# Pinned instruction order, constant matmuls at the start and moved bound work in a fused attention and FFN kernel

## Chip, core, metric

One core of one Trainium2 chip. The metric is the device time of one execution in microseconds (us). A profile gives the span from the first to the last instruction, some 1.8 us below the time (1.7 to 2.4 us).

Engines are named as in the profile: PE is TensorE, DVE is VectorE, ACT is ScalarE, SP is SyncE, which issues nearly all transfers, and POOL is GpSimd.

## The reference

```python
def _A_ref(x, k_cache, v_cache, wq, wo):       # 32 query heads, 4 kv heads, last W = 512 keys
    q = (x @ wq).reshape(B, Sq, 32, 128)...    # x is 2048 x 1024
    scores = einsum('bhqd,bhkd->bhqk', q, k) * Dh ** (-0.5)
    p = _softmax(scores, axis=-1)
    return (p @ v).reshape(B, Sq, 4096) @ wo
def _B_ref(x, w_gate, w_up, w_down):           # 1024 -> 3584 -> 1024
    return silu(x @ w_gate) * (x @ w_up) @ w_down

mod = (_silu(c) @ w_mod).reshape(...)          # sa, ca, ga, sb, cb, gb
h = _layernorm(x) * (1 + ca) + sa
x = x + ga * _A_ref(h, ...)
h = _layernorm(x) * (1 + cb) + sb
x = x + gb * _B_ref(h, ...)
```

All inputs are bf16.

## The kernel before

The 2048 rows are worked in four chunks of 512. The attention part is one loop of 128 steps, one head of one chunk each. In a step TensorE computes the scores of head `k`, the Q projection of head `k + 3`, the output of head `k - 1`, and one piece of the output projection of finished heads. Everything else hangs on a table of tasks by step: `at(k, f, ...)`. After the loop comes the FFN, chunk by chunk.

```python
def put_q(g, q_ps):                            # VectorE empties PSUM; the scores of head g need it
    t = wk.tile([P, TCW], BF16, name="qT", tag="row", bufs=5)
    nc.vector.tensor_copy(out=t, in_=q_ps)
    qT[g] = t
...
def load_rb(g):                                # 1/rowsum, written to DRAM by ScalarE's queue (r_d), read back
    for i in range(2):                         # broadcast to all partitions
        rb = wk.tile([P, 2, TCW], FP32, name="rb", tag="rb", bufs=2)
        nc.sync.dma_start(out=rb, in_=d[2 * i:2 * i + 2, :].partition_broadcast(P))
def emit_norm(g):
    for i, rb in enumerate(rinv.pop(g // 4)):
        nc.vector.tensor_tensor(out=oo, in0=oo, in1=rb, op=ALU.mult)   # oT <- oT, rb
...
def plan_ln(k, key, sc, sh):                   # layernorm of one chunk, spread over steps
    for t in range(QT):
        tt = key[1] * QT + t
        at(k + 2 * t, ln_stats, tt)            # VectorE statistics, ScalarE Ln and Exp
        at(k + 2 * t + 1, ln_rows, tt)         # VectorE: xn
        at(k + 2 * t + 2, ln_xpose, key, tt)   # transposing transfer hT <- xn on the SP queue
    for dt in range(DT):
        at(k + 11 + dt, ln_mod, key, dt, sc, sh)   # VectorE: hT <- hT * scale + shift
...
for hg in range(H // 4):                       # bound work: sums of squares of wq and k, for a check
    for i in range(2):                         # that the scores can't overflow without a row maximum
        for j in range(2):
            at(max(0, 4 * hg - 3 + 2 * i + j), bound_wq, hg, i, j)
at(6, load_k)
at(10, bound_k)                                # 16 products, one after the other
...
for k in range(NU + 1):                        # NU = 128
    if k % 4 == 2 and k + 6 < NU:
        load_wq((k + 6) // H, ((k + 6) % H) // 4)
    if k < NU: emit_s(k)
    if k + LEAD < NU: emit_q(k + LEAD)
    ...
    run_tasks(k)
    if k >= 1:
        if k % 4 == 0: emit_l(k - 1)
        emit_o(k - 1)
```

Between this source and the chip stands a scheduler. It reorders the instructions of each engine, and the transfers of the SP queue, by its own estimate of when their inputs will be ready. Each engine then works through the resulting list.

## Time and profile before

| | before |
|---|---|
| median time at first (3 runs) | 1295.99 us (1292.82 to 1296.79) |
| profiled span | 1293.1 us |
| first Q matmul / first scores matmul | 15.44 / 28.15 us |
| from first scores to the end | 1264.95 us |
| PE idle in windows of 5 us: 70-80 us / 175-185 us | 1.42 / 1.23 us |

The page says at once what the bound is. First the busy time of TensorE and its share of the span, then the shares of the chain that ended last:

```profile
PE 1274.6 (99%) x6169; PEld 575.1 (44%) x6169; DVE 653.4 (51%) x1144; ACT 454.0 (35%) x646; POOL 0.7 (0%) x6
...
PE 93%; DVE 4%; DMA 1%; issue 1%; ACT 0%; SPq 0%; DVEq 0%
```

TensorE is the bound, and in steady state a 128x512 matmul starts every 0.2158 us. This is the chain of waits, start, duration and what ran: 448 matmuls in 96.69 us.

```profile
852.56 96.69 PE gu_ps L1099 x448
```

So a change can win only the start and the few stretches in which TensorE idles. The busy time by stretches shows those (stretch, its length, then for each engine the busy us with the number of instructions in brackets, then the granted clock, DMA share and GB/s):

```profile
70.00:75.00 5.00, 4.22 (x22) 1.67 (x20) 5.00 (x39) 2.43 (x3) 0.00 (x0) 1.00 1.08 275
75.00:80.00 5.00, 4.36 (x19) 1.60 (x19) 5.00 (x9) 3.75 (x5) 0.00 (x0) 1.00 1.23 354
175.00:180.00 5.00, 3.90 (x19) 1.66 (x17) 3.65 (x8) 2.43 (x3) 0.00 (x0) 1.00 0.99 311
```

At 70-80 us VectorE is full; at 175-180 us it is not. The start, in the timeline (start us, duration us, engine, line, operation, output and inputs, forms, and the idle time before it with what ended it):

```profile
15.44 2.72 PE L878 MATMUL q_ps<-hT,wq 128*128 128x512 bf16 x6 [0.44 <-ACT hT L826]
...
18.07 2.28 PE L878 MATMUL q_ps<-hT,wq 128*128 128x512 bf16 x6
...
21.31 0.94 PE L728 MATMUL mod_ps<-siluc,wm_1_119 128*128 128x1 bf16 x32 [0.25 <-DVE modT L730]
...
23.53 4.27 PE L878 MATMUL q_ps<-hT,wq 128*128 128x512 bf16 x12
...
28.15 1.02 PE L966 MATMUL s_ps<-qT,kT 128*128 128x512 bf16 x4
```

Twelve Q matmuls run from 15.44 us, then two groups of w_mod columns, then twelve more Q matmuls, then the first scores. Six in 2.72 us with pipelined ends is 0.43 us apart, twice the steady 0.216. The Trainium skill, "TensorE: Matmul & The Clock Gate", Part 1, describes this: the array starts at half clock and gets the full one after about 3.4 us of sustained work. The granted clock that the profile prints for 10-20 us here is 1.00 all the same: no clock event was on record yet, so near the start the spacing of matmuls is the better witness. The trace also keeps the times at which the granted clock changed (views of narrow windows show them). The first such record here is a step to full clock at 19.77 us, 4.33 us after the first Q matmul. The second is a fall back to half from 23.18 to 26.60 us, and that is why the second twelve Q matmuls take 4.27 us (clock 0.82, third from the end):

```profile
20.00:25.00 5.00, 4.50 (x71) 2.74 (x70) 1.84 (x8) 1.55 (x2) 0.00 (x0) 0.82 1.03 188
```

Last, what VectorE waited for between 28 and 690 us that was a transfer (total us, times, longest us):

```profile
DVE oT L1004 <- DMA rb<-r_d: 18.8, 16, 1.7
DVE hT L829 <- DMA hT<-xn: 12.1, 5, 5.9
...
DVE xn L809 <- DMA hT<-xn: 2.1, 1, 2.1
```

With one wait of 1.3 us more these make 34 us.

### The profile page before, as it was taken

What the parts mean: (1) busy time and instruction counts of PE and PEld (TensorE: products, weight loads), DVE (VectorE), ACT (ScalarE), POOL (GpSimd) and SP (SyncE); (2) the same over time, 40 slices, a digit from 0 to 9 for tenths busy, and PEclk for the clock granted to TensorE, in tenths of its full rate; (3) what the DMA queues carried; (4) which work ended last, traced back from release to release, by engine and by line L of the source; (5) the groups of instructions that cost most, each with busy time, mean ns of one, the idle gap of its engine ahead of it and who ended that gap; (6) DMA issues with size and microseconds to landing.
All of it is one profiled execution on the core that took longest, in us unless ns stands there. A gap on an engine that the chain in (4) does not pass through costs nothing.

```text
span 1293.1 us, 15465 instructions
## 1 busy us (share of the span) xinstructions
PE 1274.6 (99%) x6169; PEld 575.1 (44%) x6169; DVE 653.4 (51%) x1144; ACT 454.0 (35%) x646; POOL 0.7 (0%) x6
## 2 busy tenths in 40 slices
PE   6999999999999999999999999999999999999998
PEld 3444444444444444444444444444444444444444
DVE  5999768975569655597654641221222211222122
ACT  3755545655455555555453441001100111011100
POOL 0000000000000000000000000000000000000000
PEclk9999999999999999999999999999999999999999
DMA  9897584665354645355447475453536445454402
GB/s 303 273 320 215 206 203 144 187 172 177 122 184 137 180 139 172 130 156 171 163 137 232 161 224 180 145 191 131 165 105 215 167 144 180 137 191 131 147 18 83
DMA packets 219939, 221.08 MB, mean 171 GB/s; under 512 B 45385, under 2 KB 205129, under 8 KB 219858
## 3 DMA queue, kind: packets, MB, share of 16 engines
q1 hardware_dynamic: 214690, 215.54, 52.6%
q10 hardware_dynamic: 5168, 4.46, 1.0%
q8 instruction: 50, 0.82, 0.2%
q14 instruction: 31, 0.25, 0.1%
HBM read 207.63 MB, written 4.47 MB: 164 GB/s over the span
## 4 chain that ended last, share of the span: by engine, by line
PE 93%; DVE 4%; DMA 1%; issue 1%; ACT 0%; SPq 0%; DVEq 0%
PE gu_ps L1099 30%; PE a_ps L1031 17%; PE d_ps L1119 15%; PE q_ps L953 15%; PE o_ps L1014 8%; PE s_ps L966 7%; DVE junk L893 1%; PE l_ps L983 1%; PE q_ps L878 1%; DVE psA L973 1%; DVE qT L855 1%; DMA rb<-r_d 1%; DVE st L793 0%; DMA hT<-xn 0%; DVE psB L975 0%
## 5 line engine op out<-in xcount | busy, mean ns | idle before, releaser
L968 ACT ACTIVATE pT<-s_ps 128x1024 bf16<-128x1024 f32 x256 | 249.0, 1028 | 8.7 <-PE s_ps L966 5.3
L1031 PE MATMUL a_ps<-wo,oT 128*128 128x512 bf16 x1024 | 242.3, 379 | 1.7 <-DVE qT L855 1.2
L953 PE MATMUL q_ps<-hT,wq 128*128 128x512 bf16 x1000 | 237.1, 380 | 0.3 <-DVE modT L730 0.3
L1104 ACT ACTIVATE sg<-gu_ps 128x512 bf16<-128x512 f32 x112 | 66.9, 597 | 460.4 <-PE gu_ps L1099 306.6
L1105 DVE TENSOR_TENSOR guT<-gu_ps,sg 128x512 bf16<-128x512 f32 x112 | 77.5, 692 | 280.8 <-ACT sg L1104 280.8
L1099 PE MATMUL gu_ps<-hT,wu 128*128 128x512 bf16 x896 | 211.8, 379 | 0.0
L1099 PE MATMUL gu_ps<-hT,wg 128*128 128x512 bf16 x896 | 211.7, 379 | 0.0
L1119 PE MATMUL d_ps<-wd,guT 128*128 128x512 bf16 (+2 forms) x952 | 194.2, 367 | 0.0
L1031 PEld LDWEIGHTS <-oT 128*128 128x128 bf16 x1024 | 99.6, 98 | 123.8 <-issue 2.8
L1016 ACT CAST oT<-o_ps 128x512 bf16<-128x512 f32 x128 | 74.3, 580 | 226.3 <-PE o_ps L1014 226.3
L953 PEld LDWEIGHTS <-wq 128*128 128x128 bf16 x1000 | 97.6, 98 | 118.3 <-issue 0.3
L1119 PEld LDWEIGHTS <-guT 128*128 128x128 bf16 x952 | 90.7, 98 | 103.1
L1099 PEld LDWEIGHTS <-wg 128*128 128x128 bf16 x896 | 87.5, 98 | 105.8
L1099 PEld LDWEIGHTS <-wu 128*128 128x128 bf16 x896 | 87.4, 98 | 106.0 <-DMA wu<-in_B_w_up_dram 0.4
L966 PE MATMUL s_ps<-qT,kT 128*128 128x512 bf16 x512 | 131.8, 379 | 0.6 <-ACT pT L968 0.6
L1014 PE MATMUL o_ps<-pT,v_sb 128*128 128x512 bf16 x512 | 131.8, 380 | 0.0
L973 DVE TENSOR_TENSOR psA<-pT 128x1024 bf16<-128x1024 bf16 x128 | 88.2, 689 | 72.5 <-ACT pT L968 72.3
L855 DVE CAST qT<-q_ps 128x512 bf16<-128x512 f32 x128 | 87.8, 688 | 52.9 <-PE q_ps L953 50.7
L1004 DVE TENSOR_TENSOR oT<-oT,rb 128x1024 bf16<-128x1024 bf16 x64 | 78.0, 1223 | 20.6 <-DMA rb<-r_d 20.5
L966 PEld LDWEIGHTS <-kT 128*128 128x128 bf16 x512 | 50.0, 98 | 61.5 <-issue 1.3
L1014 PEld LDWEIGHTS <-v_sb 128*128 128x128 bf16 x512 | 47.3, 98 | 61.7 <-issue 9.0
L975 DVE TENSOR_TENSOR psB<-psA 128x512 bf16<-128x512 bf16 x128 | 53.8, 421 | 0.6
(267 smaller groups left out, 454.2 us busy)
## 6 DMA issues: line engine op xcount, KB each, us to landing
wq<-in_A_wq_dram SPq DMA_DIRECT2D x64, 512.0 KB
rb<-r_d SPq DMA_DIRECT2D x64, 512.0 KB
wo<-in_A_wo_dram SPq DMA_DIRECT2D x64, 512.0 KB
wg<-in_B_w_gate_dram SPq DMA_DIRECT2D x56, 512.0 KB
wu<-in_B_w_up_dram SPq DMA_DIRECT2D x56, 512.0 KB
wd<-in_B_w_down_dram SPq DMA_DIRECT2D x56, 512.0 KB
wmr<-in_w_mod_dram SPq DMA_DIRECT2D x8, 1024.0 KB
out_dram<-o_sb ACTq DMA_DIRECT2D x31, 128.0 KB
```

Of the source, the lines that this page charges most:

```text
L855: nc.vector.tensor_copy(out=t, in_=q_ps)
L953: nc.tensor.matmul(q_ps, lhsT=wq_tiles[(cc, h // 4, dt // 4)][:, dt % 4, (h % 4) * P:(h % 4 + 1) * P], rhs=hT[("h1", cc)][:, dt, :], start ...
L966: nc.tensor.matmul(s_ps[:, i, :], lhsT=kT[:, kv, j * P:(j + 1) * P], rhs=qT[g], start=True, stop=True)
L968: nc.scalar.activation(out=p[:, 2 * jj:2 * jj + 2, :], in_=s_ps, func=ACT.Exp, scale=scale)
L973: nc.vector.tensor_tensor(out=a, in0=p[:, 0:2, :], in1=p[:, 2:4, :], op=ALU.add)
L1004: nc.vector.tensor_tensor(out=oo, in0=oo, in1=rb, op=ALU.mult)
L1014: nc.tensor.matmul(o_ps, lhsT=v_sb[:, kv, j, :], rhs=pT[g][:, j, :], start=(j == 0), stop=(j == WT - 1))
L1016: nc.scalar.copy(out=oT[(cc, hg)][:, hi, :], in_=o_ps)
L1031: nc.tensor.matmul(a_ps, lhsT=oT[(cc, 2 * q + i)][:, hh % 4, t * P:(t + 1) * P], rhs=wo_tiles[(cc, q, dh, i)][:, hh % 4, :], start=(hh == ...
L1099: nc.tensor.matmul(ps[:, n, :], lhsT=gu_w[(cc, fg, nm, dt // 4)][:, dt % 4, fi * P:(fi + 1) * P], rhs=hT[("h2", cc)][:, dt, :], start=(dt ...
L1105: nc.vector.tensor_tensor(out=guT[(cc, fg)][:, fi, :], in0=ps[:, 1, :], in1=g, op=ALU.mult)
L1119: nc.tensor.matmul(d_ps, lhsT=guT[(cc, f // 4)][:, f % 4, t * P:(t + 1) * P], rhs=wd_tiles[(cc, dh, f // 4)][:, f % 4, c0:c0 + w], start=( ...
```

## The change

Its intent: hold the clock of TensorE up while the first loads land; take the bound work out of chunk 0, where VectorE is full; and stop the scheduler from putting transfers, and VectorE work that waits for transfers, earlier than they can run. `keep_in_program_order` adds an order edge from an instruction to the one traced just before it on its engine. It sets the order of issue only and is no wait.

```diff
+    stage = {"dma": True, "steps": False}
+    def pin(ins, what="steps"):
+        return tc.keep_in_program_order(ins) if stage[what] else ins
+    def fetch(out, in_):                       # every load of the attention part goes through this
+        pin(nc.sync.dma_start(out=out, in_=in_), "dma")
...
+    def warm(n):                               # constants
+        for _ in range(n):
+            tc.keep_in_program_order(
+                nc.tensor.matmul(warm_ps, lhsT=ones_bf, rhs=warm_w, start=True, stop=True))
+    warm(16)
...                                             # in the first layernorm, after each transpose group:
+        warm(2)
...                                             # pinned VectorE work: bn_stats, xn, hT modulation,
-            nc.vector.tensor_tensor(out=oo, in0=oo, in1=rb, op=ALU.mult)     # bound products, norm
+            pin(nc.vector.tensor_tensor(out=oo, in0=oo, in1=rb, op=ALU.mult))
...
-                at(max(0, 4 * hg - 3 + 2 * i + j), bound_wq, hg, i, j)
-    at(6, load_k)
-    at(10, bound_k)
+                at((1 + hg % (NTC - 1)) * H + max(0, 4 * hg - 3 + 2 * i + j), bound_wq, hg, i, j)
+    at(NU - H + 2, load_k)
+    for kv in range(Hkv):
+        at(NU - H + 20 + 2 * kv, bound_k, kv)
...
+    def plan_late_ln(k, key, sc, sh):          # only for the last chunk's second layernorm
+        for t in range(QT):
+            tt = key[1] * QT + t
+            at(k + 2 * t, late_stats, tt)
+            at(k + 10 + 2 * t, ln_rows, tt)
+            at(k + 11 + 2 * t, ln_xpose, key, tt)
+        at(k + 8, late_rstd)                   # one 1/sqrt for all four row tiles, on VectorE
...
+    stage["steps"] = True
     for k in range(NU + 1):
...                                             # wq, wo and w_mod loads are also split over two steps;
...                                             # output projection and 2nd layernorm come one step later
+    stage.update(dma=False, steps=False)       # before the FFN
```

More of the change, by code (lines that the diff above doesn't have):

```diff
@@ L653, in big, with load @@
         return psp.tile(list(shape), dt, name=name, tag="s", bufs=2)
-    def load(out, in_, eng=None):
+    stage = {"dma": True, "steps": False}
[3 more added lines that the diff above has]
+        pin(nc.sync.dma_start(out=out, in_=in_), "dma")
+    def load(out, in_):
         with nc.allow_non_contiguous_dma(reason="weight slice"):
-            (eng or nc.sync).dma_start(out=out, in_=in_)
+            fetch(out=out, in_=in_)
     nc.scalar.preload_act_table_set("natural_log_exp_and_others")
@@ L666, in load_x @@
     def load_x(tt):
-        nc.sync.dma_start(out=xt[tt], in_=x2d[tt * P:(tt + 1) * P, :])
+        fetch(out=xt[tt], in_=x2d[tt * P:(tt + 1) * P, :])
     wm_tiles = {}
@@ L691, in fast_path @@
     for kv in range(Hkv):
-        nc.sync.dma_start_transpose(out=kT[:, kv, :], in_=A_k_cache[0, kv, k0:k0 + W, :])
+        pin(nc.sync.dma_start_transpose(
+            out=kT[:, kv, :], in_=A_k_cache[0, kv, k0:k0 + W, :]), "dma")
     v_sb = blkB("v_sb", [P, Hkv, WT, Dh])
@@ L704, in fast_path @@
     nc.vector.memset(eps_t, eps)
+    warm_w = const.tile([P, 512], BF16, name="warm_w")
+    nc.gpsimd.memset(warm_w, 0.5)
+    warm_ps = mm("warm_ps")
+    def warm(n):
[3 more added lines that the diff above has]
+    warm(16)
     modT = const.tile([P, 4, DT], FP32, name="modT")
@@ L742, in fast_path, with load_rows @@
     row_d = {}
-    def load_rows(vecs, part):
-        wm_rows.append([])
-        for vec in vecs:
-            t = hpool.tile([P, 4, D], BF16, name="wmr", tag="hT")
-            load(t, wm_v[:, 4 * part:4 * part + 4, vec * D:(vec + 1) * D])
-            wm_rows[-1].append(t)
+    def load_rows(vec, part):
+        t = hpool.tile([P, 4, D], BF16, name="wmr", tag="hT")
+        load(t, wm_v[:, 4 * part:4 * part + 4, vec * D:(vec + 1) * D])
+        wm_rows.append(t)
     def mod_rows(n, part):
         ps = mm("row_ps")
-        tiles = wm_rows.pop()
+        tiles = [wm_rows.pop(0) for _ in range(2)]
         for k in range(4):
@@ L766, in mod_rows @@
             d = dp.tile([4, TCW], FP32, name="row_d", tag="row_d", bufs=2)
-            nc.sync.dma_start(out=d, in_=r[0:P:32, :])
+            fetch(out=d, in_=r[0:P:32, :])
             row_d[n] = d
     def load_gate(n, k, dst):
-        nc.sync.dma_start(out=dst.rearrange("p (a b) -> p a b", a=2),
+        fetch(out=dst.rearrange("p (a b) -> p a b", a=2),
                           in_=row_d[n][k:k + 2, :].partition_broadcast(P))
@@ L776, in load_cols @@
         with nc.allow_non_contiguous_dma(reason="1024 values to columns"):
-            nc.sync.dma_start(out=dst, in_=src)
+            fetch(out=dst, in_=src)
         if add_one:
@@ L788, in fast_path, with ln_stats @@
     ln = {}
-    def ln_stats(tt):
+    def ln_stats(tt, late=None):
         st = sm.tile([P, DH, nc.vector.BN_STATS_DIM], FP32, name="st", tag="st")
         for i in range(DH):
-            nc.vector.bn_stats(out=st[:, i, :], in_=xt[tt][:, i * 512:(i + 1) * 512])
+            pin(nc.vector.bn_stats(out=st[:, i, :], in_=xt[tt][:, i * 512:(i + 1) * 512]))
+        if late is not None:
+            nc.vector.bn_aggr(out=late[:, 0:2], in_=st)
+            return
         mv = sm.tile([P, 4], FP32, name="mv", tag="mv", bufs=4)
@@ L808, in ln_norm @@
         else:
-            nc.vector.tensor_scalar(out=n, in0=xt[tt], scalar1=mv[:, 0:1], scalar2=mv[:, 2:3],
-                                    op0=ALU.subtract, op1=ALU.mult)
+            pin(nc.vector.tensor_scalar(out=n, in0=xt[tt], scalar1=mv[:, 0:1],
+                                        scalar2=mv[:, 2:3], op0=ALU.subtract, op1=ALU.mult))
         return n
@@ L821, in ln_xpose @@
             new_hT(key)
-        nc.sync.dma_start_transpose(out=hT[key][:, :, t * P:(t + 1) * P], in_=xn.pop(tt))
+        pin(nc.sync.dma_start_transpose(
+            out=hT[key][:, :, t * P:(t + 1) * P], in_=xn.pop(tt)), "dma")
     def ln_affine(key, dt, ps, sc, sh, on_act):
@@ L828, in ln_affine @@
         else:
-            nc.vector.tensor_scalar(out=hT[key][:, dt, :], in0=ps, scalar1=sc[:, dt:dt + 1],
-                                    scalar2=sh[:, dt:dt + 1], op0=ALU.mult, op1=ALU.add)
+            pin(nc.vector.tensor_scalar(out=hT[key][:, dt, :], in0=ps, scalar1=sc[:, dt:dt + 1],
+                                        scalar2=sh[:, dt:dt + 1], op0=ALU.mult, op1=ALU.add))
     def ln_mod(key, dt, sc, sh):
@@ L836, in new_hT, with late_rstd, late_stats @@
         hT[key] = hpool.tile([P, DT, TCW], BF16, name="hT", tag="hT")
+    mvl = const.tile([P, QT, 4], FP32, name="mvl")
+    def late_rstd():
+        v, y, w = (mvl[:, :, i] for i in (1, 2, 3))
+        pin(nc.vector.tensor_scalar(out=v, in0=v, scalar1=eps, scalar2=None, op0=ALU.add))
+        nc.vector.tensor_scalar(out=y.bitcast(I32), in0=v.bitcast(I32), scalar1=1, scalar2=None,
+                                op0=ALU.logical_shift_right)
+        nc.vector.tensor_scalar(out=y.bitcast(I32), in0=y.bitcast(I32), scalar1=-1.0,
+                                scalar2=float(0x5f3759df), op0=ALU.mult, op1=ALU.add)
+        for _ in range(4):
+            nc.vector.tensor_tensor(out=w, in0=y, in1=y, op=ALU.mult)
+            nc.vector.scalar_tensor_tensor(out=w, in0=w, scalar=-0.5, in1=v, op0=ALU.mult,
+                                           op1=ALU.mult)
+            nc.vector.scalar_tensor_tensor(out=y, in0=w, scalar=1.5, in1=y, op0=ALU.add,
+                                           op1=ALU.mult)
+        for t in range(QT):
+            ln[S // P - QT + t] = mvl[:, t, :]
+    def late_stats(tt):
+        ln_stats(tt, mvl[:, tt % QT, :])
+    def plan_late_ln(k, key, sc, sh):
+        for t in range(QT):
+            tt = key[1] * QT + t
[3 more added lines that the diff above has]
+        at(k + 8, late_rstd)
+        for dt in range(DT):
+            at(k + 24 + dt, ln_mod, key, dt, sc, sh)
     def plan_ln(k, key, sc, sh):
@@ L889, in bound_wq @@
     def bound_wq(hg, i, j):
-        w = wq_tiles[(0, hg, i)][:, 2 * j:2 * j + 2, :]
+        w = wq_tiles[(1 + hg % (NTC - 1), hg, i)][:, 2 * j:2 * j + 2, :]
         junk = wk.tile([P, 2, 512], BF16, name="junk", tag="psA", bufs=2)
         col = (hg * 2 + i) * 2 + j
-        nc.vector.scalar_tensor_tensor(out=junk, in0=w, scalar=1.0, in1=w, op0=ALU.mult,
-                                       op1=ALU.mult, accum_out=sq[:, col:col + 1])
+        pin(nc.vector.scalar_tensor_tensor(out=junk, in0=w, scalar=1.0, in1=w, op0=ALU.mult,
+                                           op1=ALU.mult, accum_out=sq[:, col:col + 1]))
     def load_k():
@@ L899, in load_k, with bound_k, bound_mod @@
             load(k_ld[0][:, kv], k_v[:, kv])
-    def bound_k():
-        kk = sm.tile([P, Hkv * WT], FP32, name="kk", tag="kk", bufs=1)
-        for i in range(Hkv * WT):
+    kk = const.tile([P, Hkv * WT], FP32, name="kk")
+    def bound_k(kv):
+        for j in range(WT):
+            i = kv * WT + j
             junk = wk.tile([P, Dh], BF16, name="junk", tag="psA", bufs=2)
-            src = k_ld[0][:, i // WT, i % WT, :]
-            nc.vector.scalar_tensor_tensor(out=junk, in0=src, scalar=1.0, in1=src, op0=ALU.mult,
-                                           op1=ALU.mult, accum_out=kk[:, i:i + 1])
+            src = k_ld[0][:, kv, j, :]
+            pin(nc.vector.scalar_tensor_tensor(out=junk, in0=src, scalar=1.0, in1=src,
+                                               op0=ALU.mult, op1=ALU.mult,
+                                               accum_out=kk[:, i:i + 1]))
+    def bound_mod():
         nc.vector.tensor_reduce(out=gd[:, 1:2], in_=kk, axis=AX.X, op=ALU.max)
@@ L919, in bound_final @@
         d = dp.tile([P, 4], FP32, name="gd_d", tag="gd_d", bufs=1)
-        nc.sync.dma_start(out=d, in_=gd)
+        fetch(out=d, in_=gd)
         row = wk.tile([1, P, 4], FP32, name="gd_row", tag="f32", bufs=2)
-        nc.sync.dma_start(out=row, in_=d)
+        fetch(out=row, in_=d)
         r = sm.tile([1, 8], FP32, name="gdr", tag="gdr", bufs=1)
@@ L996, in load_rb @@
             rb = wk.tile([P, 2, TCW], FP32, name="rb", tag="rb", bufs=2)
-            nc.sync.dma_start(out=rb, in_=d[2 * i:2 * i + 2, :].partition_broadcast(P))
+            fetch(out=rb, in_=d[2 * i:2 * i + 2, :].partition_broadcast(P))
             rinv[g // 4].append(rb)
@@ L1017, in emit_o, with load_wo @@
         del pT[g]
-    def load_wo(cc, q, dh):
-        for i in range(2):
-            t = blkC("wo", [P, 4, 512])
-            load(t, wo_v[:, q * HQ + 4 * i:q * HQ + 4 * i + 4, dh * 512:(dh + 1) * 512])
-            wo_tiles[(cc, q, dh, i)] = t
+    def load_wo(cc, q, dh, i):
+        t = blkC("wo", [P, 4, 512])
+        load(t, wo_v[:, q * HQ + 4 * i:q * HQ + 4 * i + 4, dh * 512:(dh + 1) * 512])
+        wo_tiles[(cc, q, dh, i)] = t
     def emit_wo(cc, q, u):
@@ L1050, in fast_path @@
         for part in range(2):
-            k = 16 * n + 8 * part + 1
-            at(k, load_rows, vecs, part)
-            at(k + 4, mod_rows, n, part)
+            k = 16 * n + 8 * part
+            at(k, load_rows, vecs[0], part)
+            at(k + 2, load_rows, vecs[1], part)
+            at(k + 5, mod_rows, n, part)
         at(16 * n + 15, load_gate, n, 0, gb_bc if n else ga_bc)
@@ L1061, in fast_path @@
             for j in range(2):
-                at(max(0, 4 * hg - 3 + 2 * i + j), bound_wq, hg, i, j)
-    at(6, load_k)
-    at(10, bound_k)
-    at(H + 2, bound_final)
+                at((1 + hg % (NTC - 1)) * H + max(0, 4 * hg - 3 + 2 * i + j), bound_wq, hg, i, j)
+    at(NU - H + 2, load_k)
+    for kv in range(Hkv):
+        at(NU - H + 20 + 2 * kv, bound_k, kv)
+    at(NU - H + 29, bound_mod)
+    at(NU + 3, bound_final)
     for g in range(3, NU, 4):
@@ L1072, in fast_path @@
         for q in range(NQ):
-            s0 = cc * H + q * HQ + HQ + 4
+            s0 = cc * H + q * HQ + HQ + 5
             for dh in range(DH):
-                at(s0 + 4 * dh - 4, load_wo, cc, q, dh)
+                for i in range(2):
+                    at(s0 + 4 * dh - 5 + i, load_wo, cc, q, dh, i)
             for u in range(2 * QT):
                 at(s0 + u, emit_wo, cc, q, u)
-        plan_ln((cc + 1) * H + 12, ("h2", cc), cb1, sb)
+        plan = plan_ln if cc < NTC - 1 else plan_late_ln
+        plan((cc + 1) * H + 13, ("h2", cc), cb1, sb)
     guT = {}
@@ L1131, in run_tasks @@
             f(*a)
+    stage["steps"] = True
     for k in range(NU + 1):
-        if k % 4 == 2 and k + 6 < NU:
-            load_wq((k + 6) // H, ((k + 6) % H) // 4)
+        if k % 4 >= 2 and 4 * (k // 4) + 8 < NU:
+            g = 4 * (k // 4) + 8
+            load_wq(g // H, (g % H) // 4, (k % 4 - 2,))
         if k < NU:
```

## The prediction

> **What bounds the kernel now.** TensorE: 99% busy on the page, 93% of the chain that ended last. In steady state a 128x512 matmul starts every 0.2158 us (chain of waits: 272 gate/up matmuls in 58.78 us). From the first scores (28.15 us) on, the stretches by window show TensorE idle in only three places: 0.7 us at 25-35, 1.42 us at 70-80, 1.23 us at 175-185 us. After 185 us all is dense but for some 5 us of tail. So the change can win only at the start and about 3.4 us of stalls.
>
> **The start.** The timeline shows the first Q matmuls cold: 12 from 15.44 to 20.3 us, 0.43 us apart; the second 12 take 4.27 us from 23.53, warm only at the end. The Trainium skill ("TensorE: Matmul & The Clock Gate", Part 1) says the array starts at half clock and reaches full clock after about 3.4 us of sustained work; 0.43 against 0.216 us agrees. 16 warm-up matmuls while TensorE idles (until 7.37 us) should lift the clock, two more after each of four transpose groups hold it. The first 12 then take 2.6-2.9 us instead of 4.9. The next step, two groups of w_mod columns (0.9 us each), needs transfers: 6.3 MB, at 316 GB/s over the first 20 us (windows); I estimate the last w_mod tile at 19-20 us, against its use at 21.3 now, so about 2 us of the gain survives. The second 12 stay partly paced by the serial hT writes (2.7 us). First scores at 25-26 us instead of 28.15: -2.4 us (1 to 3.5); near 0 if the clock falls back before 15 us.
>
> **Chunk 0.** VectorE is 100% busy from 35 to 105 us: 32 bound products on wq (1.22 us each, 39 us) and 16 on k, 3.4 us back to back at 70-73.4. That burst holds up psA and qT and costs the 1.42 us. Moved to chunks 1 to 3: -1.4 us. The 39 us are not saved, only moved.
>
> **175-185 us.** Four hT transposes go out at 161.87-169.5 us, the rb loads come behind them; VectorE waits for rb (1.74 us), does norm and modulation in one lump, and qT is late (1.23 us). Program order with a freer VectorE should finish this layernorm earlier: -1.0 us.
>
> **Costs.** 24 constant matmuls, 5 to 10 us of TensorE in mostly idle time. Chunks 1-3 get 12+12+8 products; VectorE is already 100% busy at 240-260 us without a TensorE stall and gains up to 16 us per 166; four products fall together at the start of chunk 1 (4.9 us). Strict order can block the SP queue (rb already waits for r_d 29 times, 123 us), but loads are planned 4 to 6 iterations of 5.2 us ahead. I allow +0.5 us. The late layernorm without ScalarE tables: 0, the gate/up stretch at 745-804 us is already dense.
>
> **Sum.** -2.4 -1.4 -1.0 +0.5 = -4.3 us: 1291.5 us, range 1286.5 to 1296.5. Faster by over 2%: 0.02; within 2%: 0.96; slower: 0.02. (2% would need 26 us.)
>
> **What would show it.** First Q matmuls 0.216 us apart; first scores at 25-26 us; VectorE well under 90% in 35-105 us; TensorE full at 70-80 and 175-185 us; FFN stretches (96.7 and 48.35 us) unchanged.
>
> **What would make it wrong.** The clock dropping before 15 us; first scores waiting for kT or wq because loads stay the limit; a transfer or pinned VectorE operation at the head of its queue holding up qT or wo by several us per chunk; VectorE saturation in chunks 1-3 delaying PSUM evacuation.

## The result

| | before | after |
|---|---|---|
| median of 4 runs of the same rounds | 1294.53 us | 1293.12 us (1291.92 to 1294.64) |
| ratio | | 0.9989, 95% interval 0.9967 to 1.0011 |
| profiled span | 1293.1 us | 1290.1 us |
| first Q / first scores | 15.44 / 28.15 us | 16.95 / 26.30 us |
| first scores to the end | 1264.95 us | 1263.80 us |

Ratios are the mean time of one kernel's fast runs over that of the other's of the same rounds, so not quite the ratio of the medians beside them. The interval holds 1, so the gain is not clear of noise. The gain of the profiled pair, 3.0 us, is larger than that of the timed runs, 1.4 us. The spans of the four runs after are 1290.1, 1291.3, 1291.3 and 1292.9 us at mean clocks of 0.999, 0.997, 0.998 and 0.996: the profiled one was the fastest, at the highest clock.

The page after, the same two lines:

```profile
PE 1271.4 (99%) x6073; PEld 577.4 (45%) x6193; DVE 653.1 (51%) x1159; ACT 433.7 (34%) x625; POOL 1.2 (0%) x7
...
PE 95%; SPq 2%; DMA 1%; DVE 1%; issue 1%; DVEq 0%
```

The stretches that answer to those of before, and one that is new:

```profile
70.00:75.00 5.00, 4.95 (x26) 2.08 (x25) 5.00 (x8) 4.16 (x6) 0.00 (x0) 1.00 0.80 232
75.00:80.00 5.00, 5.00 (x36) 2.02 (x34) 3.67 (x8) 1.71 (x4) 0.00 (x0) 1.00 0.38 122
175.00:180.00 5.00, 5.00 (x25) 2.26 (x24) 4.31 (x7) 2.43 (x3) 0.00 (x0) 1.00 0.59 148
760.00:765.00 5.00, 3.25 (x16) 1.32 (x15) 3.96 (x10) 0.60 (x1) 0.00 (x0) 1.00 1.03 339
```

Both stalls, of chunks 0 and 1, are gone (4.95 of 5 is a missing record: PE has 6073 matmuls on the page after and PEld 6193 weight loads). A stall of 1.75 us has come in the FFN, where before showed a full 5.00. What VectorE waited for, 28 to 690 us:

```profile
DVE gdr L990 <- DMA gd_row<-gd_d: 1.1, 1, 1.1
DVE oT L1069 <- DMA rb<-r_d: 1.1, 1, 1.1
DVE modT L800 <- DMA modT<-row_d: 0.3, 1, 0.3
```

That is 2.5 us instead of 34. The start:

```profile
12.80 0.95 PE L751 MATMUL mod_ps<-siluc,wm_0_113 128*128 128x1 bf16 x32 [1.18 <-DMA wm_0_113<-in_w_mod_dram]
...
16.95 1.53 PE L938 MATMUL q_ps<-hT,wq 128*128 128x512 bf16 x6
...
18.40 1.46 PE L938 MATMUL q_ps<-hT,wq 128*128 128x512 bf16 x6
...
21.09 0.95 PE L751 MATMUL mod_ps<-siluc,wm_1_119 128*128 128x1 bf16 x32 [0.53 <-DMA wm_1_119<-in_w_mod_dram]
...
23.15 2.80 PE L938 MATMUL q_ps<-hT,wq 128*128 128x512 bf16 x12
...
26.30 1.02 PE L1031 MATMUL s_ps<-qT,kT 128*128 128x512 bf16 x4
```

The first Q matmuls now run at full pace, but they begin 1.5 us later than before. In TensorE's new order the transposes stand behind a group of w_mod columns that waits 1.18 us for its tile, and behind constants. The granted clock fell here too, to half from 13.69 to 17.10 us by the clock records: 0.87 over 10-15 us and 0.79 over 15-20 us.

```profile
10.00:15.00 5.00, 3.60 (x82) 3.19 (x81) 2.53 (x14) 2.12 (x5) 0.00 (x0) 0.87 1.10 348
15.00:20.00 5.00, 5.00 (x39) 2.76 (x37) 1.09 (x2) 1.55 (x2) 0.00 (x0) 0.79 1.10 348
```

Then the next columns wait for their transfer until 21.09 us, against a use at 21.31 us before. What the warm clock gained ahead of that point is lost at it; only the second twelve Q matmuls (2.80 us instead of 4.27) are a gain.

The new stall in the FFN, first the SP queue and then TensorE in the timeline of after, then the SP queue of before in the same place:

```profile
751.39 6.76 SPq L846 DMA_TRANSPOSE hT<-xn  x4
...
758.24 0.53 SPq L664 DMA_DIRECT2D wu<-in_B_w_up_dram  x1
...
762.27 1.04 PE L1168 MATMUL gu_ps<-hT,wu 128*128 128x512 bf16 x4 [1.75 <-DMA wu<-in_B_w_up_dram]
```

```profile
738.22 5.91 SPq L822 DMA_TRANSPOSE hT<-xn  x2
744.64 0.93 SPq L657 DMA_DIRECT2D wd<-in_B_w_down_dram  x2
...
749.38 6.21 SPq L822 DMA_TRANSPOSE hT<-xn  x2
```

Four transposing transfers stand as one block of 6.76 us ahead of a `wu` load after; before they were two pairs with loads between.

### The profile page after: what moved, and what is told of

Same layout as the page of the kernel before. It is cut to its first block, busy times and chain, and to the rows that moved or that the text cites. A ratio compares the mean times of both kernels' runs of the same rounds, so it can differ in the third digit from the quotient of the medians.

```text
span 1290.1 us, 15319 instructions
## 1 busy us (share of the span) xinstructions
PE 1271.4 (99%) x6073; PEld 577.4 (45%) x6193; DVE 653.1 (51%) x1159; ACT 433.7 (34%) x625; POOL 1.2 (0%) x7
## 4 chain that ended last, share of the span: by engine, by line
PE 95%; SPq 2%; DMA 1%; DVE 1%; issue 1%; DVEq 0%
PE gu_ps L1168 29%; PE a_ps L1095 17%; PE q_ps L1018 17%; PE d_ps L1188 15%; PE o_ps L1079 9%; PE s_ps L1031 8%; SPq L664 1%; PE l_ps L1048 1%; SPq L703 1%; DMA hT<-xn 0%; DMA wq<-in_A_wq_dram 0%; DMA wu<-in_B_w_up_dram 0%; PE row_ps L777 0%; DVE guT L1174 0%; DVE xn L833 0%
## 5 line engine op out<-in xcount | busy, mean ns | idle before, releaser
L1033 ACT ACTIVATE pT<-s_ps 128x1024 bf16<-128x1024 f32 x256 | 252.0, 1026 | 72.8 <-PE s_ps L1031 67.3
L1095 PE MATMUL a_ps<-wo,oT 128*128 128x512 bf16 x972 | 238.9, 379 | 2.6
L1069 DVE TENSOR_TENSOR oT<-oT,rb 128x1024 bf16<-128x1024 bf16 x64 | 75.4, 1218 | 1.5 <-DMA rb<-r_d 1.5
```

The lines of the kernel that those rows point to most:

```text
L1033: nc.scalar.activation(out=p[:, 2 * jj:2 * jj + 2, :], in_=s_ps, func=ACT.Exp, scale=scale)
L1069: pin(nc.vector.tensor_tensor(out=oo, in0=oo, in1=rb, op=ALU.mult))
L1095: nc.tensor.matmul(a_ps, lhsT=oT[(cc, 2 * q + i)][:, hh % 4, t * P:(t + 1) * P], rhs=wo_tiles[(cc, q, dh, i)][:, hh % 4, :], start=(hh == ...
```

## Experiments

Twelve kernels ran. The table has what the argument needs of each; names beginning with b are edits of the kernel before, those with a of the kernel after. "Idle" is the PE idle time in the windows of 5 us that show more than 0.2 us of it, from 35 to 735 us (attention) and from 735 to 1240 us (FFN). For the kernel before it leaves out the 0.13 us at 180-185 us, which the 1.23 us above count. "DVE waits" is the sum of VectorE's waits for transfers, 28 to 690 us.

| kernel | first Q | first scores | span | scores to end | idle, attention | idle, FFN | DVE waits | median, ratio to before (95% interval) |
|---|---|---|---|---|---|---|---|---|
| before | 15.44 | 28.15 | 1293.1 | 1264.95 | 2.52 | 0 | 34.3 | |
| after | 16.95 | 26.30 | 1290.1 | 1263.80 | 0 | 1.75 | 2.5 | 1293.12, 0.9989 (0.9967-1.0011) |
| a_nopins | 17.57 | 27.64 | 1303.1 | 1275.46 | 7.94 | 2.05 | 60.5 | 1306.65, 1.0079 (1.0062-1.0095) |
| a_dvepins | 16.61 | 28.09 | 1293.5 | 1265.41 | 0 | 1.97 | 2.4 | 1294.21, 0.9976 (0.9953-1.0000) |
| a_dmapins | 17.25 | 27.46 | 1291.5 | 1264.04 | 0 | 1.76 | 41.4 | 1293.37, 0.9978 (0.9956-1.0001) |
| b_pins | 15.87 | 27.81 | 1290.7 | 1262.89 | 0.56 | 0 | 0 | 1292.93, 0.9974 (0.9953-0.9994) |
| b_bound | 15.60 | 26.14 | 1296.9 | 1270.76 | 5.08 | 1.23 | 57.8 | 1298.42, 1.0009 (0.9992-1.0026) |
| a_bound0 | 17.75 | 27.94 | 1293.0 | 1265.06 | 0.99 | 1.81 | 1.2 | 1295.35, 0.9987 (0.9969-1.0004) |
| a_nowarm | 15.50 | 27.98 | 1292.5 | 1264.52 | 0 | 2.47 | 1.6 | 1294.96, 0.9987 (0.9971-1.0004) |
| b_warm | 16.63 | 25.63 | 1294.9 | 1269.27 | 5.66 | 0.85 | 39.3 | 1297.06, 1.0002 (0.9985-1.0019) |
| a_hold | 19.46 | 30.09 | 1293.7 | 1263.61 | 0 | 1.85 | 1.4 | 1294.10, 0.9980 (0.9960-1.0000) |
| a_plainln | 18.46 | 27.86 | 1290.8 | 1262.94 | 0 | 0.73 | 1.6 | 1291.85, 0.9960 (0.9938-0.9981) |
| a_pinffn | 17.68 | 27.59 | 1297.4 | 1269.81 | 0 | 5.74 | 0.2 | 1299.41, 1.0018 (1.0000-1.0036) |
| a_both | 18.91 | 27.89 | 1291.2 | 1263.31 | 0 | 1.51 | 1.7 | 1293.50, 0.9979 (0.9961-0.9998) |

The kernels ran in groups on the same chip with their own runs of the kernel before, whose median was 1296.90 us (a_nopins, b_bound, a_nowarm, b_warm), 1297.13 (a_dvepins, a_dmapins, a_bound0, a_pinffn) and 1296.09 us (the rest). All results were correct. The profiles of before and after are from rounds of their own, so a comparison of another profile with them is one of single executions in different rounds. The stalls hold up in it: first scores to the end, less the two idle columns, is 1261.8 to 1262.8 us in ten of the fourteen. a_dvepins, a_pinffn, b_bound and a_nopins lie above that (1263.4 to 1265.5), all but b_bound with a stretch of half clock behind a stall.

### The pins

**a_nopins**: the kernel after, no pins but those of the constants.

```diff
     def pin(ins, what="steps"):
-        return tc.keep_in_program_order(ins) if stage[what] else ins
+        return ins
```

> The kernel after, with every pin but those of the constant matmuls taken away, so the scheduler orders transfers and VectorE again. Theory A (the pins are worth nothing by themselves; the gain is warm-up and moved bound work, and the late 1.75 us stall at 760-762 us in the FFN is due to the late layernorm): first scores about 26.3 us, no stall at 70-80 or 175-185, the FFN stall stays, span within 1 us of 1290.1. Rival (the pins took the stall at 175-185 us away): a stall of 1 us or more comes back in chunk 0 to 2.

Measured: 1306.65 us, slower than before by 0.8% in the same rounds, with a span 13.0 us above that of the profile after. Theory A is refuted: without pins the rest of the change loses. Which part of the rest loses is not shown: the moved bound work alone and the constants alone leave the time the same (b_bound, b_warm below), and the loads split over two steps never ran alone. Of the 11.66 us more from first scores to the end, stalls make 8.24. The largest stall shows the mechanism. First the waits in 183-196 us, then the timeline:

```profile
DVE hT L854 <- DMA hT<-xn: 4.9, 1, 4.9
PE q_ps L1018 <- DVE qT L914: 3.4, 1, 3.4
```

```profile
177.24 6.76 SPq L846 DMA_TRANSPOSE hT<-xn  x3
...
187.01 2.67 DVE L854 TENSOR_SCALAR hT<-hT,modT 128x512 bf16<-128x512 bf16 x8 [4.94 <-DMA hT<-xn]
...
190.20 0.69 DVE L914 CAST qT<-q_ps 128x512 bf16<-128x512 f32 x1
...
190.94 3.31 PE L1018 MATMUL q_ps<-hT,wq 128*128 128x512 bf16 x8 [3.44 <-DVE qT L914]
```

Three transposing transfers held the queue for 6.76 us. The modulation of hT needs them, and it stands in VectorE's list ahead of a qT copy whose input is long there. VectorE idles 4.94 us, works off eight modulations and a psA, and only then empties the PSUM bank that TensorE waits for. The Trainium skill says of these engines that they are strict FIFO ("TensorE: Matmul & The Clock Gate", "Architectural detail", engine queue depths), and this trace agrees: the copy that was ready did not pass the one that was not. The stall also costs twice. After 3.44 us of idle the eight Q matmuls take 3.31 us instead of 1.89, half clock again (granted 0.66 over 190-195 us); the same page, "Why this matters for your kernels", warns of idle gaps over about 3 us. Less was enough in a_dvepins: after 1.97 us of idle that ended at 763.91 us the clock was at half from 763.97 to 767.38 us.

From this came theory B: it is VectorE operations at the head of the list, waiting for a transfer, that stall TensorE.

**a_dvepins** and **a_dmapins**: one kind of pin each.

```diff
# a_dvepins: transfers unpinned (fetch and both transposing transfers)
-        pin(nc.sync.dma_start(out=out, in_=in_), "dma")
+        nc.sync.dma_start(out=out, in_=in_)
# a_dmapins: VectorE unpinned
-    stage["steps"] = True
```

> The kernel after, with the VectorE pins kept and the transfer pins taken away. Theory B (formed after the first four runs: what stalls TensorE in chunks 0 to 3 is a VectorE operation whose transfer has not landed, placed ahead of the qT copy in an engine that works in order; pinning VectorE's order removes it): VectorE waits for transfers 28-690 us sum to under 10 us (2.5 in the profile after, 60 without any pin), stalls of TensorE there under 1 us in all, span 1290 to 1292. Rival C (the transfers' order is what matters: loads that VectorE waits for come late in the queue): waits of 20 us or more, stalls of 3 us or more, span 1294 or longer.

> The kernel after, with the transfer pins kept and the VectorE pins taken away. Theory B: VectorE waits for transfers 28-690 us stay at 20 us or more and TensorE stalls of 3 us or more come back, span 1295 to 1303. Rival C: waits under 10 us, span within 1 us of 1290.1.

Measured: each kind alone removes every stall of the attention part. With VectorE's order pinned the waits fall to 2.4 us, as theory B said (its span of 1293.5 us is over the range, with first scores at 28.09 us). With only the transfers pinned VectorE still waits 41.4 us for transfers, and yet TensorE loses nothing. Theory B in its simple form falls here, and rival C guessed the waits wrong. It had the stalls right; its range for the span is missed by 0.4 us, through the start (first scores 1.16 us later than after's, and only 0.24 us more from there on). The waits in a_dmapins:

```profile
DVE oT L1069 <- DMA rb<-r_d: 29.7, 29, 3.3
...
DVE gdr L990 <- DMA gd_row<-gd_d: 3.6, 1, 3.6
DVE st L814 <- DMA x<-in_A_x_dram: 3.4, 4, 1.6
```

They are short: 29 waits for rb make 29.7 us, and the longest of all is 3.6 us. I read this as follows: a wait of VectorE costs time only when it is longer than the slack of the copy behind it, and either kind of pin keeps it below. No run tests this slack directly. The length alone does not decide: in the kernel before a wait of 5.9 us for hT that ended at 278.4 us cost TensorE nothing, while one of 3.0 us that ended at 173.0 us came just ahead of the stall at 175 us.

**b_pins**: the kernel before with the pins alone; the same edits of `fetch` and `pin` as in the change, nothing else of it.

```diff
# all loads through fetch(), transposing transfers and the listed VectorE work through pin(), as above
+    stage["steps"] = True
     for k in range(NU + 1):
...
+    stage.update(dma=False, steps=False)
     for cc in range(NTC):
```

> The kernel before, with only the two kinds of pins (transfers throughout the attention part, the listed VectorE work in its loop); no constants, bound work in chunk 0, loads in the old portions, old layernorm at the end. If the pins alone take away the waits of VectorE for transfers: these waits sum to under 6 us over 28-690 us (34 before), the stall at 175-185 us goes, the stall behind the burst on k stays at 0.5 to 1.4 us, first scores at 28 us, span 1291 to 1292.5. If the pins need the other parts (the bound work moved, smaller portions of loads): stalls of 3 us or more, span 1294 or longer.

Measured: no wait of VectorE for a transfer at all, no stall at 175-185 us, 0.56 us left behind the burst on k, no stall in the FFN, first scores at 27.81 us, span 1290.7, ratio 0.9974 with an interval below 1. It keeps from first scores to the end 2.06 us over the kernel before; the stalls fell by 1.96 us. In the profiles the pins alone do as much as the whole change.

### The bound work

**b_bound**: the kernel before with the bound work moved, nothing else.

```diff
# bound_wq reads the tiles of chunk 1 + hg % 3, bound_k is cut into four, its end is bound_mod; then
-                at(max(0, 4 * hg - 3 + 2 * i + j), bound_wq, hg, i, j)
-    at(6, load_k)
-    at(10, bound_k)
-    at(H + 2, bound_final)
+                at((1 + hg % (NTC - 1)) * H + max(0, 4 * hg - 3 + 2 * i + j), bound_wq, hg, i, j)
+    at(NU - H + 2, load_k)
+    for kv in range(Hkv): at(NU - H + 20 + 2 * kv, bound_k, kv)
+    at(NU - H + 29, bound_mod)
+    at(NU + 3, bound_final)
```

> The kernel before, with only the bound work moved to chunks 1 to 3 (k in four pieces). Theory A (both stalls of chunk 0 come from a saturated VectorE): TensorE full at 65-85 and at 170-190 us, first scores still at 28.15 us, span 1290.3 to 1290.8. Rival (the stall at 175-185 us comes from the order of the transfers): only the 1.42 us at 70-80 us go, span 1291.6 and the stall at 175-185 us stays.

Measured: both theories missed. The stall at 70-80 us is gone, but others came at 55-60, 80-85, 95-105 and 180-185 us. The idle time rose from 2.52 to 5.08 us, and the waits of VectorE for transfers from 34 to 58 us. Part of this may lie between the rounds: the runs of the kernel before beside this one had spans of 1294.3 to 1296.5 us, its profile 1293.1. The stall at 80-85 us, in the waits of 78-86 us:

```profile
DVE hT L829 <- DMA hT<-xn: 3.4, 1, 3.4
...
PE q_ps L957 <- DVE qT L855: 1.6, 1, 1.6
```

VectorE was free (1.59 of 5 us busy in that stretch) and stood still. I read this as: a freer VectorE in the scheduler's order reaches the operations that wait for transfers sooner, and waits longer. It is not isolated, as the whole list was scheduled anew. That first scores came at 26.14 us here, without constants and from almost the same first Q time as before (15.60 us), shows how much the clock at the start varies between executions: its first six Q matmuls were 0.43 us apart, the rest 0.216.

**a_bound0**: the kernel after with the bound work back in chunk 0.

```diff
-        w = wq_tiles[(1 + hg % (NTC - 1), hg, i)]...
+        w = wq_tiles[(0, hg, i)]...
-                at((1 + hg % (NTC - 1)) * H + max(0, 4 * hg - 3 + 2 * i + j), bound_wq, hg, i, j)
+                at(max(0, 4 * hg - 3 + 2 * i + j), bound_wq, hg, i, j)
# load_k at 6, bound_k and bound_mod at 10, bound_final at H + 2, as before
```

> The kernel after, pins and warm-up kept, with the bound work back in chunk 0 as before. If the saturation of VectorE in chunk 0 costs time even in program order: a stall of 1 to 2 us at 65-80 us behind the burst on k, span 1291.3 to 1292.5. If only waits for transfers cost time (theory B in its strict form): no stall there, span 1290.1 within 0.6.

Measured: 0.45 us of stall at 70-75 and 0.54 at 80-85 us, so 0.99 us in all, and 1.26 us more from first scores to the end than the kernel after. Under pins the burst does cost about 1 us, below the 1.42 us of before and at the lower end of the expectation. The span of 1293.0 us is 2.9 us longer; the other 1.64 us lie in the start.

### The constants

**a_nowarm**: the kernel after without constants. **b_warm**: the kernel before with the 24 constants.

```diff
# a_nowarm
-        for _ in range(n):
+        for _ in range(0):
# b_warm: warm_w, warm_ps, warm() and warm(16) as in the change, and
+        warm(2)              # after each transpose group of the first layernorm
```

> The kernel after, without its 24 constant matmuls; all else kept. Theory A (the start is set by the arrival of the last w_mod tile, 21.1 us in the profile after, and the warm clock only shortens the 12 Q matmuls behind it, 2.80 against 4.27 us): first scores at about 27.8 to 28.2 us instead of 26.30, span about 1.5 to 1.9 us longer (1291.6 to 1292.0). Rival (the warm-up is worth the whole start, its first 12 Q matmuls too): first scores at 29.5 us or later. Rival 2 (the warm-up does nothing, the pins made the start shorter): first scores still at 26.3 us. The windows 70-80 and 175-185 us stay full in all three.

> The kernel before, with only the 24 constant matmuls added. Theory A: first scores at 26.0 to 26.5 us instead of 28.15, the stalls at 70-80 us (1.42) and 175-185 us (1.23) stay, span 1291 to 1291.7. Rival (the clock does not hold without pinned order of the loads): first scores at 28 us, span 1293.

Measured for a_nowarm: first scores at 27.98 us as theory A said, span 1292.5 us, which is 2.4 us more than after's and over the expected range; 0.7 us of it is a longer FFN stall. Its timed ratio, 0.9987, is that of the kernel after, 0.9989: in the timed runs the constants are worth nothing that shows.

Measured for b_warm: first scores at 25.63 us, a head start of 2.52 us, and no gain: span 1294.9 us, ratio 1.0002. The scheduled lists explain what to compare. From the first scores on, the lists of TensorE, VectorE, ScalarE and the SP queue are the same as before; they differ only in rows ahead of the first scores. Yet TensorE's idle time in the attention part rose from 2.52 to 5.66 us and 0.85 us came in the FFN, together 3.99 us, more than the head start. These are the stretches of the attention part that grew most, as in the table of before:

```profile
70.00:75.00 5.00, 3.48 (x17) 1.01 (x15) 5.00 (x21) 1.92 (x4) 0.00 (x0) 1.00 1.14 331
120.00:125.00 5.00, 4.12 (x31) 1.54 (x30) 5.00 (x12) 4.32 (x8) 0.00 (x0) 1.00 0.09 17
180.00:185.00 5.00, 3.91 (x19) 1.78 (x19) 5.00 (x10) 1.12 (x2) 0.00 (x0) 1.00 0.56 150
```

Same orders, earlier start, longer waits: in this execution of the unpinned kernel the head start was given back. How much of the longer waits comes from the earlier start and how much from the other rounds, one profile can't say; the ratio of 1.0002, within the rounds, shows that nothing of it was left.

**a_hold**: more constants, to hold the clock.

```diff
-        warm(2)
+        warm(4)
# and after each of the first two w_mod column groups
+        if half == 0:
+            warm(4)
```

> The kernel after, with 4 constant matmuls instead of 2 after each transpose group and 4 more after each of the first two w_mod column groups (40 in all). Theory D (in most executions TensorE is too little busy between 7 and 15 us, the clock falls to half for a window somewhere in 13-28 us, and the warm-up's gain at the start is lost; only held busy does it keep the clock): all Q matmuls 0.216 us apart, first scores at 25.6 to 26.5 us, mean clock 0.998 or more in all runs, time 1 us below the kernel after's. Rival (more constants delay the real work by more than the clock gives): first scores at 27 us or later with the clock held.

Measured: theory D failed. The twelve constants after the last transposes ran in one row and held up the first Q matmuls:

```profile
15.95 3.67 PE L725 MATMUL warm_ps<-warm_w,ones_bf 128*128 128x512 bf16 x12
19.46 2.75 PE L940 MATMUL q_ps<-hT,wq 128*128 128x512 bf16 x12
...
25.93 3.80 PE L940 MATMUL q_ps<-hT,wq 128*128 128x512 bf16 x12
```

First Q at 19.46 and first scores at 30.09 us, the latest of all. And the clock fell even so: after two groups of w_mod columns (64 matmuls of one column) the next twelve Q matmuls took 3.80 us (half clock from 24.63 to 28.05 us). In a_both, with the same constants, it held (2.79 us for the same twelve, granted clock 1.00 from 5 to 30 us) and first scores still came only at 27.89 us. So the rival was right: the constants cost more real work than they give.

Over the fourteen profiles, the eight with the 24 constants of the change have first scores at 27.31 us on average; the four without constants (before, a_nowarm, b_bound, b_pins) at 27.52 us. I can't tell these apart: single values go from 25.63 to 28.15 us.

The clock records of the traces show what the constants did. Each stretch between two changes of the clock is a multiple of 3.41 us. The ten kernels with constants are at full clock by 4.2 to 6.9 us, but nine of them (all but a_both) fall back to half for one or two such windows between 12.7 and 20.2 us. The four without get there at 16.5 to 19.8 us, and three of them (all but b_bound) fall back for one window between 22.1 and 26.8 us. So the constants brought the full clock some 10 us earlier and moved the fall rather than prevented it. A count over all traces fits how full a window was: with 0.2158 us for a matmul of 512 columns and the others by their columns, the 17 windows of 3.41 us at full clock ahead of a fall (that in the tail left out) were filled to 9 to 39%, the other 5,100 or so to 39% or more. The 64 matmuls of one column count for almost nothing in it: the window of a_hold that holds them (21.22-24.63 us) is 31% full, that of a_both with most of them (19.93-23.34 us) 46%. This is worked out from the traces, not tested by a run.

### The stall in the FFN

**a_plainln**: the kernel after with the old layernorm for the last chunk. **a_pinffn**: the pins kept on through the FFN of chunk 0.

```diff
# a_plainln
-        plan = plan_ln if cc < NTC - 1 else plan_late_ln
+        plan = plan_ln
# a_pinffn
-    stage.update(dma=False, steps=False)
     for cc in range(NTC):
+        if cc == 1:
+            stage.update(dma=False, steps=False)
         for fg in range(NFG):
```

> The kernel after, with the last chunk's layernorm planned as before (statistics by ScalarE tables, four row tiles one after the other) instead of the late one. If the late layernorm made the 1.75 to 2.2 us stall at 760 us, by letting four hT transposes go as one batch ahead of a wu load: the stall is gone or under 0.5 us, and the span from first scores to the end is 1.7 us shorter than the kernel after's (1263.8 us). Rival (the stall comes from program order in the attention part, which leaves the loads of the FFN late): a stall of 1 us or more between 740 and 800 us stays. First scores may be anywhere from 26.3 to 28 us, with the clock.

> The kernel after, with the pins kept on through the FFN of chunk 0, where the late layernorm falls. If the 1.75 us stall at 760 us comes from four hT transposes that the scheduler let go as one batch ahead of the wu load: in program order they go out one every two steps (about 6.9 us apart), the stall goes, span 1288.3 to 1288.8. If it comes from the late layernorm as such: a stall of 1 us or more at 755-790 us stays.

Measured for a_plainln: the wait for `wu` is gone. A stall of 0.73 us is left at 755-760 us, behind a VectorE operation that waits for hT, slightly over what was expected. From first scores to the end it is 0.86 us shorter than the kernel after, not 1.7. Its time has the best ratio of all, 0.9960. So the late layernorm caused the block of four transfers, and about 1.0 of the 1.75 us of stall; why the other 0.73 us come with the old layernorm too, and not in the kernel before, stays open.

Measured for a_pinffn: pins are not good everywhere. The stall at 760 us is gone, but now whole runs of loads stand in line behind a transfer that can't go yet, and TensorE idles 5.74 us in the FFN, 3.52 us of it at 785-790 us. The SP queue, and the wait of TensorE in 780-830 us:

```profile
784.87 1.29 SPq L846 DMA_TRANSPOSE hT<-xn  x1
786.26 1.09 SPq L664 DMA_DIRECT2D wg<-in_B_w_gate_dram  x2
```

```profile
PE gu_ps L1168 <- DMA wg<-in_B_w_gate_dram: 3.9, 1, 3.9
```

The `wg` load went out only at 786.26 us, directly behind the transpose, and TensorE waited 3.9 us for it. The expected gain was wrong: the stall moved and grew. The transpose at the head of the queue had waited 14.4 us for xn. That the queue holds until the head can go fits the Trainium skill, "DMA: Bandwidth & Descriptors", "Anatomy of one DMA" (of transfers that GpSimd issues, but the sentence is on DMA engines in general): waits for semaphores happen on the issuing sequencer, not in the DMA engines.

### The two findings together

**a_both**: a_plainln with the constants of a_hold.

> The kernel after, with the old layernorm for the last chunk and the constants of a_hold (40 matmuls): the version that the two theories point to. Both right: no stall over 0.5 us from first scores to the end but for the tail, first scores at 26.3 us, span 1288 to 1289, time 1290 to 1291, about 0.5% under the kernel before. If one of the two is wrong: span 1290 to 1292.

Measured: 1293.50 us, ratio 0.9979 with an interval just below 1. It is faster than before, but not shown to be faster than a_plainln or b_pins, whose intervals overlap its own. The constants put first Q at 18.91 us, and 1.51 us of stall in the FFN stayed behind VectorE (`guT`).

## Why the prediction was right or wrong

The time was right: 1291.5 us with 1286.5 to 1296.5, measured 1293.12 us, and "within 2%" as forecast. That rests on one sound step: TensorE's idle time was counted first, and there were only about 3.4 us of it after the start. For the single terms the hit says little: the range also held the median of before (1294.53 us), so that no gain at all would have been in it. The sum was -4.3 us, the timed runs show -1.4 us (not clear of zero) and the profiled pair -3.0 us. Term by term:

- **"First scores at 25-26 us instead of 28.15: -2.4 us"**: mis-sized. The profiled run has -1.85 us, the other profiles with constants 25.6 to 28.1 us, and without constants the time is the same (a_nowarm, 0.9987). The prediction named both reasons as risks. The two matmuls after each transpose group did not hold the clock: it fell back (0.87 and 0.79 granted over 10-20 us), and the last w_mod tile came at 21.1 us, not at 19-20. It missed that constants and the new order of TensorE would put the first Q matmul 1.5 us later.
- **"That burst holds up psA and qT and costs the 1.42 us. Moved to chunks 1 to 3: -1.4 us"**: the burst is a real cost only in part. Moved alone, it made the kernel no faster (b_bound: 5.08 us of stalls). Under pins the move is worth 0.99 us of stall (a_bound0).
- **"Program order with a freer VectorE should finish this layernorm earlier: -1.0 us"**: right in size (1.23 us) and right about program order. A freer VectorE without it did not help (b_bound), and program order without a freer VectorE did (b_pins, a_bound0).
- **"I allow +0.5 us"** for strict order: on the safe side. In the attention part the transfers' queue waited 338 us for r_d instead of 123 and TensorE lost nothing; the loads are planned steps ahead, as the prediction argued. The FFN is not pinned in the change; pinned there, order does cost (a_pinffn). These are the SP queue's own waits, before and after:

```profile
SPq L997 <- DMA r_d<-rinv: 123.2, 29, 6.8
```

```profile
SPq L664 <- DMA r_d<-rinv: 337.9, 30, 20.0
```

- **"The late layernorm without ScalarE tables: 0"**: wrong: this step failed, not only its size. There is a stall of 1.75 us at 760 us behind four transposing transfers that go as one block. With the old layernorm the wait for `wu` is gone and 0.73 us of stall is left (a_plainln), so about 1.0 us is the late layernorm's. "FFN stretches (96.7 and 48.35 us) unchanged" did hold: those of chunks 1 to 3 are the same; the stall is in the gate/up stretch of chunk 0, ahead of them.

Taken from the two profiles, the stalls account for -2.52 + 1.75 = -0.77 of the -1.15 us from first scores to the end.

What stays open: how much of the 0.5% spread between executions is the clock at the start. The spans of the kernel after go with its mean clock, but those of a_hold (1291.7 to 1293.7 us) and a_both (1290.3 to 1294.8) only roughly do. Nor was b_pins run in the same rounds as the kernel after, so that it is better than the whole change is likely from the profiles but not shown by times.

## What to carry to other kernels

Where engines work through their lists in order, look at what the helper engine waits for and at what stands behind that wait. Total waiting says little (41 us cost nothing, one wait of 4.9 us cost about 5 with the half clock behind it), and freeing an engine without fixing its order need not help. A head start counts only if the stages behind it can take it: compare the idle time after the start as well as the time of the start. Pin order where loads are planned steps ahead of their use, and not where one late transfer would hold a row of loads.

## What the Trainium skill lacked or had wrong

- "TensorE: Matmul & The Clock Gate", Part 1: about 3.4 us of sustained work raise the clock, in windows that run freely. The kernel before agrees: dense Q matmuls from 15.44 us, full clock at 19.77 us, so one window of 3.41 us lies within them. What the page does not give is how full a window must be to keep the clock; here the windows ahead of a fall were filled to 9 to 39%, the others to 39% or more.
- The same page says nothing of matmuls of one column as activity. In a_hold 64 of them in 2.1 us were followed by half clock (twelve Q matmuls in 3.80 us); in a_both, in the same order, the clock held (2.79 us), with a window that was 46% full instead of 31%.
- The same page advises to warm up ahead when a matmul is to be timed. It does not say that constants take their place in a kernel's list: 12 of them took 3.67 us and the first Q matmul moved from 16.95 to 19.46 us.
- No page that I used says that a scheduler's order and a strict FIFO together turn a late transfer into a stall of TensorE two engines away (a_nopins: 4.94 us of VectorE waiting, 3.44 us of TensorE, then half clock for eight matmuls).
